# Key/value stage of a transformer block: the two LN1 norms and transposes of a tile pair placed behind products three and five of the value group instead of both behind product six

## The chip, the cores and the metric

The kernel runs on one core of one Trainium2 chip. The metric is device time in microseconds (us). The kernel before took 736.23 us (median of 3 runs, 735.11 to 737.95). The stage of interest is some 70 us long.

Engines are named as in the profile: PE (TensorE matmul), PEld (its weight load), DVE (VectorE), ACT (ScalarE), POOL (GpSimd), SP (the engine whose queue issues nearly all DMAs here).

## The reference

The block is a pre-norm linear attention followed by a pre-norm gated MLP, for 2048 tokens of width 1024, in bf16. Only the first lines matter here:

```
x = A_x                                    # [1, 2048, 1024]
h = x + A_ref(layernorm(x), wqkv, wo)      # linear attention, 32 heads
h2 = h + B_ref(layernorm(h), W_gate, W_up, W_down)

# in A_ref: q, k, v from layernorm(x) @ wqkv
pk = phi(k);  kv = sum over tokens of pk^T v;  z = sum of pk
```

## The kernel before

The tokens are 16 tiles of 128. The key/value stage works on pairs of tiles. For each pair it makes a product of the normalised tiles with the key weights and one with the value weights, each in seven half-size products (a Strassen-like scheme of sums and differences). The order of the seven in a group is P1, P7, P6, P2, P5, P4, P3; `hook(i)` stands behind the i-th product issued, so "behind product three" means hook 3.

```python
def sgroup(...):                       # one group; cuts marked ...
    prod(a, X(0, 0), W(0, 0), True, "P1");  ...;  hook(1)
    prod(f, SX(2), TW(2), True, "P7");      ...;  hook(2)
    prod(b, SX(1), TW(1), False, "P6");     ...;  hook(3)
    prod(a, X(1, 0), W(1, 0), False, "P2"); ...;  hook(4)
    prod(c, SX(0), TW(0), False, "P5")
    ident_act(sc, bank(c), ...)             # ACT copies a bank out
    s22 = e22(...);  s22[0]()               # value group: first value addition, DVE
    hook(5)
    prod(b, X(1, 1), TW(3), False, "P4")
    s21 = e21(...);  s21[0]()               # value group: second value addition, DVE
    hook(6)
    prod(c, SX(3), W(1, 1), False, "P3");   ...;  hook(7)
```

`SX` are sums and differences of the two transposed tiles of a pair, which DVE makes one pair ahead of its use:

```python
def x_sums(p, part=None):              # DVE, four operations of 128x512
    if part != 1: add(2, xb(0, 0), xb(0, 1), ALU.subtract, ...)  # reads both tiles of the pair
    ...
```

A tile is normalised by DVE into `xn`, transposed by a DMA into `xnT`, and its input slot is loaded again:

```python
def T1d(st):
    dma_t(sl_tx[k], xnT[:, :, st * P:(st + 1) * P], xn[:, k, :], ...)   # SP: DMA transpose
    if st + NX1 < NST:
        load_x1(st + NX1)                                               # SP: next x tile into the freed slot
def norm(st):
    if st < NST:
        ln1_norm(st)                   # DVE, 128x1024
        T1d(st)
def norms(p):
    norm(2 * p)
    norm(2 * p + 1)
```

The loop, with what stands in which hook:

```python
for p in range(NP_):
    # key group p: hook 1 ln1_stats(2p+6); hook 5 x_sums(p+2, 0) and ACT statistics; hook 6 x_sums(p+2, 1)
    k_group(p, hooks)
    if p + 2 < NP_:
        def v3(...):                   # behind product three of value group p+2
            ...
            if p == 0:
                x_sums(1)
                norm(6)
        def v5(p=p):                   # behind product five
            if p == 0:
                norm(7)
            ...                        # ACT statistics of tile 2p+9
        def v6(p=p, nq=nq):            # behind product six
            if p > 0:
                norms(p + 3)
            kvaccs(p)                  # 16 accumulating matmuls of 129 columns
            ...
        v_group(p + 2, {2: v2, 3: v3, 5: v5, 6: v6})
```

So the first pair (tiles 6 and 7) already had the new order. The pairs of p = 1 to 4 had both norms behind product six, and the next key group wants their transposed tiles behind its product five.

## Time and profile before

| what | before | view |
|---|---|---|
| span, granted clock | 734.9 us, 1.00 | the page |
| PE / DVE / ACT / POOL busy | 98 / 76 / 48 / 14% | the page |
| PE busy in the odd 14 us of the stage | 13.43 of 14.00 us | windows |
| a round on PE (accumulation to accumulation) | 13.16 to 13.21 us, but 13.61 in round 1 and 13.96 in round 3 | timeline |
| first transpose of the pair in that round | issued 64.07 us, landed after 3.1 us | timeline, DMA |
| second transpose | issued 65.97 us, landed after 4.8 us | timeline, DMA |

The sixteen narrow matmuls of an accumulation (128x129, from RE) are a good mark on PE's timeline. Successive starts of them give the rounds: 35.51, 49.12, 62.29, 76.25, 89.41 and 102.62 us, so rounds 1 to 5 take 13.61, 13.17, 13.96, 13.16 and 13.21 us.

PE's timeline of the kernel before (start, duration, engine, line, operation, tiles, count; in brackets the idle time before and who ended it):

```profile
62.29 1.10 PE L710 MATMUL ps<-RE 128*128 128x129 bf16 x16
63.44 0.81 PE L710 MATMUL ps<-RAB,RH 128*128 128x512 bf16 x3
64.09 1.03 PE L710 MATMUL ps<-RAB 128*128 128x512 bf16 x4
...
71.32 1.04 PE L710 MATMUL ps<-RW,RWG 128*128 128x512 f16 x4
72.81 1.02 PE L710 MATMUL ps<-RW,RWG 128*128 128x512 f16 x4 [0.45 <-DVE RWG L931]
...
76.25 1.10 PE L710 MATMUL ps<-RE 128*128 128x129 bf16 x16
```

The third line, at 64.09, is the first matmul of the next key group. The odd round is round 3 (62.29 to 76.25). In it PE stands idle for 0.45 us before a product that reads DVE's pair sum (L931), and the product before it started late as well.

The timeline of all engines of the kernel before, the lines of the two norms (L778, L838), the value additions (L1073), SP's issues (SPq) and the pair sum:

```profile
62.30 0.69 DVE L1073 TENSOR_TENSOR RE<-ps,RX 128x512 bf16<-128x512 f32 x1 [0.46 <-ACT RX L715]
62.91 0.68 DVE L1073 TENSOR_TENSOR RE<-ps,RXH 128x512 bf16<-128x512 f32 x1
63.51 0.54 DVE L778 TENSOR_SCALAR RXH<-RE,mv,rstd 128x1024 bf16<-128x1024 bf16 x1
63.96 0.54 DVE L838 TENSOR_SCALAR RXH<-RE,s 128x1024 bf16<-128x1024 bf16 x1
64.07 1.23 SPq L545 DMA_TRANSPOSE RAB<-RXH  x1
65.35 0.58 SPq L541 DMA_DIRECT2D RE<-in_A_x_dram  x1
65.97 1.23 SPq L545 DMA_TRANSPOSE RAB<-RXH  x1
...
70.84 0.42 DVE L931 TENSOR_TENSOR RWG<-RAB 128x512 f16<-128x512 bf16 x1 [0.81 <-DMA RAB<-RXH]
```

Two things are to be seen. The second norm is done at 64.50, but its transpose is issued only at 65.97, because SP first issues the other transpose and a load. And DVE stands 0.81 us at 70.84, released by the DMA of that transpose: it was ready at 70.03, which is +5.9 us on the round's clock. The chain of waits of the kernel before (start, duration, what) runs through just this:

```profile
65.97 4.84 DMA RAB<-RXH
70.82 0.02 issue
70.84 0.42 DVE RWG L931
```

### The profile page before, as it was taken

To read this page: it belongs to the slowest core of one execution; us is meant where nothing else is said; L and a number is where in the kernel's file an instruction comes from. 1 tells how busy PE (TensorE), PEld (TensorE's weight loads), DVE (VectorE), ACT (ScalarE), POOL (GpSimd) and SP (SyncE) were. 2 spreads that over 40 slices of the span, in tenths; PEclk is the share of its full clock that TensorE was granted. 3 is DMA by queue.
4 is the path that set the end of the run, shared out by engine and by line. 5 is a ranking of instruction groups with operands and counts; after the bars stand their busy time and mean duration, and the time that the engine had idled before them with its cause. 6 is when DMAs were issued, how large, how long until landed. Compare 5 with 4: busy or idle time off the path is not lost.

```text
span 734.9 us, 11505 instructions
## 1 busy us (share of the span) xinstructions
PE 720.8 (98%) x4253; PEld 363.2 (49%) x4311; DVE 561.6 (76%) x976; ACT 352.0 (48%) x614; POOL 103.7 (14%) x169
## 2 busy tenths in 40 slices
PE   8999999999999999999999999999999999999998
PEld 3444444344444444444444666754444444447766
DVE  7878877898775999898997769865757575667594
ACT  4877666764832456777754100135454544521000
POOL 1311100000450112132320003400000000000052
PEclk9999999999999999999999999999999999999999
DMA  9644154024999889888969999982323242327892
GB/s 313 202 91 83 29 142 157 3 30 75 214 228 260 234 258 272 241 243 256 300 198 305 318 247 336 311 263 79 101 71 109 63 116 58 100 92 245 246 314 87
DMA packets 191880, 133.93 MB, mean 182 GB/s; under 512 B 51664, under 2 KB 173776, under 8 KB 191824
## 3 DMA queue, kind: packets, MB, share of 16 engines
q1 hardware_dynamic: 191152, 132.54, 63.6%
q8 instruction: 34, 0.56, 0.3%
q10 hardware_dynamic: 672, 0.66, 0.3%
q14 instruction: 22, 0.18, 0.1%
HBM read 96.47 MB, written 25.17 MB: 166 GB/s over the span
## 4 chain that ended last, share of the span: by engine, by line
PE 82%; DVE 9%; DMA 3%; issue 2%; ACT 2%; SPq 1%; POOL 1%; POOLq 0%; DVEq 0%; ACTq 0%
PE ps L710 82%; DMA RW<-in_B_W_down_dram 1%; DVE RAB L796 1%; DVE RE L1171 1%; ACT RX L789 1%; DMA RX<-h_scr 1%; DVE st L724 1%; DMA RAB<-RXH 1%; DVE RX L793 1%; SPq L541 1%; DVE RX L1012 1%; DVE RO L1289 1%; POOL rstd L734 0%; DVE RW L906 0%; ACT ps L715 0%
## 5 line engine op out<-in xcount | busy, mean ns | idle before, releaser
L715 ACT ACTIVATE ps<-ps 128x512 f32<-128x512 f32 x172 | 100.1, 582 | 213.5 <-PE ps L710 162.0
L710 PE MATMUL ps<-RC,RO 128*128 128x512 f16 x672 | 154.3, 379 | 0.0
L710 PE MATMUL ps<-RH,RWG 128*128 128x512 bf16 x447 | 105.6, 379 | 0.1
L710 PEld LDWEIGHTS ps<-RC,RO 128*128 128x128 f16 x672 | 65.7, 98 | 79.5 <-ACT ps L715 0.5
L1345 DVE TENSOR_TENSOR RAB<-ps,RAB 128x512 bf16<-128x512 f32 x56 | 38.6, 689 | 71.9 <-PE ps L710 71.9
L710 PE MATMUL ps<-RC,RWG 128*128 128x512 f16 x320 | 76.8, 379 | 0.3 <-ACT ps L715 0.3
L1341 DVE TENSOR_TENSOR RE<-ps,RE 128x512 bf16<-128x512 f32 x112 | 74.2, 684 | 1.6 <-PE ps L710 0.7
L710 PEld LDWEIGHTS ps<-RH,RWG 128*128 128x128 bf16 x448 | 43.9, 98 | 52.6
L710 PE MATMUL ps<-RW,RAB 128*128 128x256 f16 (+3 forms) x412 | 66.8, 318 | 1.5 <-DVE RAB L1423 1.0
L1423 POOL TENSOR_TENSOR RE<-RE,RX 128x512 f32<-128x512 f32 x16 | 23.1, 1473 | 307.5 <-DMA RX<-h_scr 307.5
L715 ACT ACTIVATE RE<-RE 128x512 bf16<-128x512 bf16 x56 | 35.1, 627 | 65.0 <-DVE RE L1341 64.4
L710 PE MATMUL ps<-RH,RO 128*128 128x512 bf16 (+1 forms) x228 | 55.3, 379 | 3.0 <-DVE RE L1341 1.6
L710 PE MATMUL ps<-RW,RE 128*128 128x512 bf16 x243 | 56.6, 380 | 1.5 <-DVE RXH L1195 0.7
L710 PE MATMUL ps<-RAB 128*128 128x512 bf16 (+2 forms) x268 | 57.6, 351 | 0.4
L715 ACT ACTIVATE RE<-ps 128x512 f32<-128x512 f32 x64 | 37.6, 597 | 35.4 <-PE ps L710 35.0
L710 PEld LDWEIGHTS ps<-RW,RAB 128*128 128x128 bf16 (+1 forms) x414 | 40.4, 98 | 25.8 <-DVE RAB L1423 1.3
L710 PEld LDWEIGHTS ps<-RC,RWG 128*128 128x128 bf16 (+1 forms) x320 | 30.0, 98 | 40.2 <-ACT ps L715 6.2
L1289 DVE TENSOR_TENSOR RO<-RWG 128x1024 f16<-128x1024 bf16 x54 | 39.7, 736 | 4.7 <-DMA RWG<-in_B_W_up_dram 4.7
L1423 DVE TENSOR_TENSOR RE<-ps,RE 128x512 f32<-128x512 f32 x40 | 27.0, 687 | 18.9 <-PE ps L710 15.6
L715 ACT ACTIVATE RAB<-ps 128x512 bf16<-128x512 f32 x56 | 33.4, 596 | 14.7 <-PE ps L710 13.6
L710 PEld LDWEIGHTS ps<-RH,RO 128*128 128x128 f16 (+1 forms) x256 | 24.2, 98 | 31.8 <-DVE RE L1341 2.2
L710 PEld LDWEIGHTS ps<-RAB 128*128 128x128 bf16 (+1 forms) x274 | 26.3, 98 | 25.2 <-ACT RAB L856 1.1
(138 smaller groups left out, 994.0 us busy)
## 6 DMA issues: line engine op xcount, KB each, us to landing
RWG<-in_B_W_gate_dram SPq DMA_DIRECT2D x28, 512.0 KB, 5.0
RWG<-in_B_W_up_dram SPq DMA_DIRECT2D x28, 512.0 KB, 5.9
RW<-in_B_W_down_dram SPq DMA_DIRECT2D x14, 512.0 KB, 6.1
t_scr<-RW SPq DMA_DIRECT2D x14, 512.0 KB, 3.5
RE<-in_A_x_dram SPq DMA_DIRECT2D x23, 256.0 KB, 3.5
RW<-l_scr SPq DMA_DIRECT2D x13, 448.0 KB, 6.3
l_scr<-RX SPq DMA_DIRECT2D x7, 768.0 KB, 4.4
RW<-in_B_W_down_dram SPq DMA_DIRECT2D x12, 384.0 KB, 5.0
```

The source lines that it names most:

```text
L541: return PL.add(eng, lambda e: e.dma_start(dst_ap, src_ap), reads=reads, writes=writes, slot=slot, name=name)
L710: lambda e: e.matmul(out_ap, lhsT, rhs, start=start, stop=stop, skip_group_check=skip),
L715: PL.add("act", lambda e: e.activation(out=dst, in_=src, func=func), reads=reads, writes=writes, name=name)
L724: PL.add("dve", lambda e: e.bn_stats(out=st6[:, k, c * 6:(c + 1) * 6], in_=src_full[:, c * BCH:(c + 1) * BCH]), reads=[src_chunk_bufs[c]], ...
L789: PL.add("act", lambda e: e.activation(out=Et[:, k, :], in_=src, func=ACTF.Exp), reads=[src_buf], writes=[B_E[k]], name=name + "_exp")
L793: PL.add("dve", lambda e: e.tensor_scalar(out=Et[:, k, :], in0=Et[:, k, :], scalar1=1.0, scalar2=1e-6, op0=ALU.min, op1=ALU.add), reads=[] ...
L796: PL.add("dve", lambda e: e.scalar_tensor_tensor(out=dst_ap, in0=src, scalar=C1, in1=Et[:, k, :], op0=ALU.add, op1=ALU.max), reads=[src_bu ...
L1012: PL.add("dve", lambda e: e.tensor_tensor(out=s_, in0=p_, in1=s_, op=ALU.add), reads=[pb], writes=[sb_], name=name + "_add")
L1289: PL.add(eng, lambda e: e.tensor_tensor(out=tb(j, u), in0=f0(u), in1=f1(u), op=ALU.subtract), reads=[B_w[i + x] for x in r] + ([B_T[k + x] ...
L1341: PL.add("dve", lambda e: e.tensor_tensor(out=dst, in0=src, in1=ftmp[:, w, :], op=ALU.add), reads=[bsrc, B_s5[w]], writes=[bdst], name=name)
L1345: PL.add("dve", lambda e: e.tensor_tensor(out=dst, in0=a_, in1=b_, op=ALU.mult), reads=reads, writes=[wr], name=name)
L1423: PL.add(eng, lambda e: e.tensor_tensor(out=dst, in0=in0, in1=in1, op=op), reads=reads, writes=writes, name=name)
```

## The change

The intent: finish the norms earlier in the value group, so that the transposes start earlier, and fill DVE's wait for ACT ahead of the first value addition. No operation is added or removed.

```diff
                     if p == 0:
                         x_sums(1)
                         norm(6)
+                    else:
+                        norm(2 * p + 6)
 
                 def v5(p=p):
-                    if p == 0:
-                        norm(7)
+                    norm(2 * p + 7)
                     B = 2 * p + 9
 ...
                 def v6(p=p, nq=nq):
-                    if p > 0:
-                        norms(p + 3)
                     kvaccs(p)
```

## The prediction

> What bounds the kernel now. TensorE. The page gives PE 98% busy, DVE 76%, ACT 48%, POOL 14%. In the key/value stage (about 36 to 116 us of the 734.9 us span) the windows view shows PE busy 19.4 to 20.0 us of every 20 us and DVE 14.5 to 16.3. One round (key group, value group, accumulation) repeats on PE every 13.14 to 13.21 us (starts at 50.93, 64.09, 78.05, 91.21, 104.42), except one that takes 13.96 us. So there is little to gain but 0.8 us.
>
> The chain of waits and the timeline show the odd round. DVE makes two norms behind product six at 63.51 and 63.96 us (0.54 us each). SP issues the first transpose at 64.07 (1.23 us of issue), the load after it at 65.35 (0.58), the second transpose only at 65.97; it lands 4.84 us later, at 70.82 (minimum and median of these transposes 3.0 and 3.2 us). The pair sum of the next key group, ready to start at about 70.03, waits 0.81 us for it, and PE then stands at the product that reads the sum.
>
> What the change does. Nothing is added or removed: four pairs of norms with transposes and loads come earlier. The first pair has this order already. The first norm moves in front of the first value addition (L1073). There DVE now stands idle 0.36 to 0.48 us per round, waiting for ACT's copy, so the norm (0.45 us start to start) fills that hole. The second norm goes between the two value additions and delays the second by about 0.45 us. That addition releases a PSUM bank which the next key group needs only at its third product's copy, some 2 us later, and its value tile is read two pairs later; I count no PE time for it. The statistics are ready: POOL's last operation on them ends near 58.2 us, the norm would run at about 61.8.
>
> First norm 63.51 to about 61.9, issue 64.07 to about 62.4; second norm 63.96 to about 63.0, but SP is then busy until about 64.3, so the second issue moves from 65.97 to about 64.3, 1.6 us earlier. Even a landing of 4.84 us would end at about 69.2, before 70.03. The wait of 0.81 us should vanish, and with it 0.7 to 0.8 us of PE. The Trainium skill, "DMA: Bandwidth & Descriptors" (Anatomy of one DMA, there for GpSimd's path), puts a transfer's fixed part at about 2 us; this trace shows a floor too (3.0 us), so only an earlier issue helps.
>
> The other rounds show no such wait, so I expect 0 to 0.8 us in total, at most about 1.5 in executions with two late landings: about -0.6 us of 736.23; the three runs spread over 735.11 to 737.95.
>
> Predicted: 735.6 us, range 734.0 to 737.3. Chances: faster by over 2% 0.01, within 2% 0.98, slower by over 2% 0.01.
>
> What would show it: all rounds 13.1 to 13.2 us on PE; no DVE wait on the transposed tile; second transposes issued 1.6 us earlier; DVE's wait for ACT before the first value addition nearly gone; second value addition 0.5 us later with no new PE wait.
>
> What would make it wrong: the 4.84 us landing was chance and after has its own; the earlier loads slow the second transpose; the later second addition holds a bank and PE waits for ACT's copy, some 0.3 us per round, making it slower by about 1 us.

## The result, and the profile after

The changed kernel took 735.6 us (median of 6 runs, 734.91 to 737.83), the kernel before 736.35 us in its 6 runs (735.11 to 737.95). The ratio was 0.9994, with a 95% interval of 0.9976 to 1.0013. A ratio here is the mean time of one kernel's fast runs over that of the other's of the same rounds, so it is not quite the ratio of the medians. By time alone, no difference seen: the interval contains 1. A later set of runs (below) gave 0.9985, interval 0.9972 to 0.9998.

The profiled execution of the changed kernel happened to be the slowest of its six (737.83 us), and its span is 1.2 us longer than that of before. The stage must therefore be read by itself. PE's timeline of the changed kernel:

```profile
64.77 1.10 PE L710 MATMUL ps<-RE 128*128 128x129 bf16 x16
65.71 1.02 PE L710 MATMUL ps<-RAB,RH 128*128 128x512 bf16 x4
66.57 1.03 PE L710 MATMUL ps<-RAB 128*128 128x512 bf16 x4
...
73.56 1.94 PE L710 MATMUL ps<-RW,RWG 128*128 128x512 f16 x8
...
77.92 1.10 PE L710 MATMUL ps<-RE 128*128 128x129 bf16 x16
```

Round 3 now takes 13.15 us (64.77 to 77.92), and the two products that were torn apart in before run as one line of eight matmuls. All five rounds: 13.37, 13.17, 13.15, 13.16 and 13.21 us. The timeline of all engines, the lines that answer to those above:

```profile
64.24 0.54 DVE L778 TENSOR_SCALAR RXH<-RE,mv,rstd 128x1024 bf16<-128x1024 bf16 x1
64.78 0.69 DVE L1073 TENSOR_TENSOR RE<-ps,RX 128x512 bf16<-128x512 f32 x1
64.80 1.23 SPq L545 DMA_TRANSPOSE RAB<-RXH  x1
65.39 0.54 DVE L838 TENSOR_SCALAR RXH<-RE,s 128x1024 bf16<-128x1024 bf16 x1
65.84 0.68 DVE L1073 TENSOR_TENSOR RE<-ps,RXH 128x512 bf16<-128x512 f32 x1
66.08 0.58 SPq L541 DMA_DIRECT2D RE<-in_A_x_dram  x1
66.70 1.23 SPq L545 DMA_TRANSPOSE RAB<-RXH  x1
...
72.43 0.41 DVE L931 TENSOR_TENSOR RWG<-RAB 128x512 f16<-128x512 bf16 x1
```

The first norm fills the hole before the first value addition, which has no bracket any more. On the round's clock (zero at 66.57) the second transpose is issued at +0.13 us instead of +1.88. It lands at +3.7 us, over 2 us before it is wanted, and the pair sum waits for nothing. The windows view of 14 us around the round (length, then PE, PEld, DVE, ACT and POOL busy with counts, clock, DMA share, GB/s), first of before, then of after:

```profile
64.00:78.00 14.00, 13.43 (x73) 5.95 (x72) 10.87 (x25) 10.31 (x21) 1.78 (x5) 1.00 0.42 76
```

```profile
64.00:78.00 14.00, 14.00 (x79) 6.39 (x78) 11.57 (x26) 10.90 (x22) 1.96 (x5) 1.00 0.34 76
```

Where, then, did the 1.2 us of span come from? The first accumulation starts at 38.23 us in after and at 35.51 in before (+2.72). The five rounds take 66.06 us instead of 67.11 (-1.05: 0.81 in round 3 and 0.24 in round 1; the latter is scatter and not the change, since a repeat of the kernel before also had 13.36 us there). The rest of the program takes 631.8 us instead of 632.3 (-0.5). The start is the culprit, before any moved norm: in the changed kernel's profiled execution PE stood 1.90 us for the first norm (0.77 in before), and then ran with a lower granted clock. The windows from 8 to 18 us, before and then after:

```profile
8.00:18.00 10.00, 9.82 (x64) 4.93 (x64) 9.00 (x19) 5.65 (x12) 1.46 (x3) 1.00 1.09 355
```

```profile
8.00:18.00 10.00, 9.48 (x54) 4.82 (x55) 8.93 (x21) 4.73 (x9) 1.65 (x3) 0.83 1.09 357
```

A repeat of the changed kernel began its first accumulation at 35.90 us, so this late start is not a property of the change.

### The profile page after: what moved, and what is told of

Its sections match the earlier page's. It is cut to its first block, busy times and chain, and to the rows that moved or that the text cites. A ratio compares the mean times of both kernels' runs of the same rounds, so it can differ in the third digit from the quotient of the medians.

```text
span 736.1 us, 11563 instructions
## 1 busy us (share of the span) xinstructions
PE 725.6 (99%) x4311; PEld 364.0 (49%) x4311; DVE 561.1 (76%) x976; ACT 352.3 (48%) x614; POOL 105.5 (14%) x169
## 4 chain that ended last, share of the span: by engine, by line
PE 85%; DVE 8%; ACT 2%; DMA 2%; SPq 1%; issue 1%; POOL 0%; DVEq 0%; POOLq 0%; ACTq 0%
PE ps L710 84%; DVE RAB L1423 2%; DMA RW<-in_B_W_down_dram 1%; DVE RAB L796 1%; SPq L545 1%; ACT RX L789 1%; DVE RE L1171 1%; DMA RE<-in_A_x_dram 1%; DVE RX L793 1%; SPq L541 1%; DVE RO L1289 0%; ACT ps L715 0%; ACT RXH L748 0%; DVE RX L1012 0%; DVE RE L1423 0%
## 5 line engine op out<-in xcount | busy, mean ns | idle before, releaser
L710 PE MATMUL ps<-RW,RAB 128*128 128x256 f16 (+3 forms) x414 | 66.9, 318 | 1.3 <-DVE RAB L1423 0.8
L710 PE MATMUL ps<-RH,RO 128*128 128x512 bf16 (+1 forms) x256 | 61.3, 380 | 0.9 <-DVE RE L1341 0.9
L710 PE MATMUL ps<-RAB 128*128 128x512 bf16 (+2 forms) x274 | 59.3, 357 | 0.1
```

What stands on the lines that cost most here:

```text
L710: lambda e: e.matmul(out_ap, lhsT, rhs, start=start, stop=stop, skip_group_check=skip),
```

## The experiments

Theory: the second transpose lands at the edge of the moment when it is wanted, and PE pays for what is over. Rivals: the one late landing was chance and the change did nothing, or the gain has another source. A second question arose on the way: why is it always round 3? All profiled executions but that of late (a run described below) are collected in this table. Times marked + or - are us from the zero of round 3 (first matmul of the next key group); the sum wants both transposes at +5.9.

| kernel | second transpose issued | instruction fetch starts | second transpose landed | DVE wait | round 3 |
|---|---|---|---|---|---|
| before | +1.88 | +3.8 | +6.7 | 0.81 | 13.96 |
| before_again | +1.88 | +3.6 | +6.5 | 0.55 | 13.71 |
| second_only | +1.29 | +3.5 | +6.4 | 0.52 | 13.67 |
| loads_last | +1.27 | +3.4 | +5.9 | none | 13.15 |
| before_later | +1.88 | +4.4 | +7.3 | 1.34 | 14.50 |
| before_fetch | +1.88 | -1.3 | +5.4 | none | 13.16 |
| after | +0.13 | +3.8 | +3.7 | none | 13.15 |
| after_again | +0.14 | +3.9 | +3.7 | none | 13.15 |
| first_only | +0.14 | +2.9 | +3.7 | none | 13.16 |
| after_fetch | +0.80 | -0.5 | +4.2 | none | 13.16 |
| after_hit2 | +0.15 | +4.1 | +3.7 | none | 13.15 |
| after_hit4 | +0.14 | +0.3 | +4.3 | none | 13.15 |
| best | -0.48 | +4.0 | +2.7 | none | 13.16 |

The column of the fetch needs a word. The DMA view lists, beside the data queue, queues of kind "instruction"; that of the kernel before over the whole span (packets, MB, share of the 16 engines):

```profile
q8 instruction: 34, 0.56, 0.3%
q14 instruction: 22, 0.18, 0.1%
```

The Trainium skill, "Runtime: NRT & Kernel Launch" (Instruction fetch mechanics), says that an engine's instruction memory is refilled in blocks of 16 KiB, 256 instructions, through a DMA queue of its own. The numbers agree with q8 being PE's: the trace has 34 packets of 16 KB, and the page counts 4311 weight loads, each with a matmul, so 8622 instructions or 33.7 blocks. The table has q8's fetch. Its start was read by narrowing the window of the DMA view until the packet fell into 0.1 us. The other queue, q14, fetches 8 KB at a time, and did no such harm where it met a transpose: in best one of its fetches started 2.4 us after a transpose's issue (36.99 us), which landed after 3.65 us.

### before_again and after_again: is it chance?

The same two programs, profiled and timed once more, five rounds each.

> The kernel before, run and profiled again. Theory (the second transpose of a pair lands at the edge of its need; only a late landing costs PE time): some of the rounds that begin near 51, 64, 78 and 91 us may show a DVE wait of 0.1 to 1 us on the transposed tile, and a round of 13.15 us on PE is longer by just that wait; rounds without it take 13.14 to 13.21 us. Rival 1 (the 4.84 us landing was one accident): all landings near 3.2 us, no such wait. Rival 2 (systematic): the same round waits about 0.8 us again. Time against before: same, within 0.2%.

> The changed kernel again. Theory: no DVE wait on the transposed tile in any round, all PE rounds of the stage 13.14 to 13.21 us, second transpose issued about 0.13 us after the next key group's first matmul (1.88 us in before). Time 0.0 to 0.8 us under before (ratio 0.999 to 1.000), too little to be clear of the spread. Rival (the added wait of the second value addition costs PE time): rounds longer than 13.21 us.

Measured: before_again 736.54 us (6 runs; before 736.37, 11 runs), ratio 1.0005, interval 0.9992 to 1.0018. Round 3 again, and only round 3, had the wait: 13.71 us, with this line in the waits of DVE from 60 to 75 us:

```profile
DVE RWG L931 <- DMA RAB<-RXH: 0.5, 1, 0.5
```

after_again 735.38 us (5 runs), ratio 0.9985, interval 0.9972 to 0.9998; rounds 13.36, 13.15, 13.15, 13.16 and 13.20 us, no wait on the transposed tile. So the late landing is not an accident: two of two traces of before have it in the same round (rival 2 of before_again's text), and none of two of the changed kernel. The gain seen on PE is 0.55 to 0.8 us; the ratio's interval (0.15 to 2.1 us) holds that and is not finer.

### first_only: which half of the change does it?

```diff
                         norm(6)
+                    else:
+                        norm(2 * p + 6)
 ...                                     # v5 as before
                 def v6(p=p, nq=nq):
                     if p > 0:
-                        norms(p + 3)
+                        norm(2 * p + 7)
```

> Only the first norm of the pair moved (behind product three); the second stays behind six. Theory (the second transpose is held back by SP issuing the first transpose and the load, 1.23 + 0.67 us, not by its norm): second transpose issued at 0.1 to 0.2 us after the next key group's first matmul, as with both moved (before: 1.88), no wait on the transposed tile. Rival (its own norm holds it): issued near 1.3 to 1.9 us.

Measured (one look, 734.92 us): second transpose issued at +0.14 us, as with both moved; no wait; round 3 13.16 us. SP's timeline in it:

```profile
62.33 1.23 SPq L545 DMA_TRANSPOSE RAB<-RXH  x1
...
64.22 1.23 SPq L545 DMA_TRANSPOSE RAB<-RXH  x1
```

The second transpose was held back by SP's issue of the first one and of the load, not by its own norm. In this one trace, the half of the change that moves the second norm is worth nothing.

### second_only and loads_last: the same time from SP's side

second_only moves the second norm alone (behind product five); the first stays behind six, and the transposes change places. loads_last leaves the norms where before had them, and issues both loads behind both transposes.

```diff
 # second_only
-                    if p == 0:
-                        norm(7)
+                    norm(2 * p + 7)
 ...
                     if p > 0:
-                        norms(p + 3)
+                        norm(2 * p + 6)
```

```diff
 # loads_last
         def norms(p):
-            norm(2 * p)
-            norm(2 * p + 1)
+            for st in (2 * p, 2 * p + 1):
+                if st < NST:
+                    ln1_norm(st)
+                    T1d(st, False)            # transpose without the load
+            for st in (2 * p, 2 * p + 1):
+                if st + NX1 < NST:
+                    load_x1(st + NX1)
```

> Only the second norm moved (behind product five), the first stays behind six, so the two transposes change places. Theory (SP issues them one after the other with a load between, so the later of the two is issued 1.9 us after the first): first issue about 0.6 us before the next key group's first matmul, second about 1.2 to 1.3 us after it (before: 1.88), so at most a small wait in the third round (0 to 0.3 us), or none.

> Norms where before had them; the two loads of x are issued behind both transposes instead of one between them. Theory: second transpose issued about 1.3 us after the next key group's first matmul instead of 1.88 in the rounds that load; the wait in the third round shrinks from 0.5 to 0.8 us to 0 to 0.3 us. Rival (only the norms' place matters): wait as in before.

Measured (one look each, 737.12 and 737.55 us): the later transposes were issued at +1.29 and +1.27 us, as expected. The wait was 0.52 us in second_only, more than the 0 to 0.3 expected, since the landing stretched to 5.1 us; in loads_last there was none, the landing at +5.9 being just in time. So an earlier issue did not by itself bring an earlier landing: with issues at +1.88, +1.29 and +1.27 the landing came at +6.5 to +6.7, +6.4 and +5.9, always 2.5 to 2.9 us after the start of the fetch. The fetch is not the whole of it: second_only and loads_last had the same issue and fetches 0.1 us apart, yet landed 0.5 us apart. They differ in the place of the loads and in when the first transpose was issued (-0.61 and -0.01); which of these matters was not tested.

### late: what does a later transpose cost?

```diff
                 if p > 0 and A < NST:
                     ln1_stats(A)
+                if p > 1:
+                    norms(p + 2)          # in the next key group, behind its product one
 ...
                 def v6(p=p, nq=nq):
-                    if p > 0:
-                        norms(p + 3)
                     kvaccs(p)
```

> Both norms and transposes put later instead of earlier: behind the statistics in the next key group (after its product one), about 2.1 us later on DVE than in before where statistics stand there. Theory (landing has under 1 us to spare, and every us beyond goes to PE one to one): the sum waits about 2.3 us in each of the two rounds that also load x, 1.7 us in the next, under 0.5 us in the last, so 6 us slower in all (4 to 8), ratio about 1.008, with PE waiting for the sum. Rival (transposes are off the path, 0.8 us of the odd round had another cause): within 1 us of before, PE rounds unchanged.

Measured: 740.26 us (5 runs; before 736.37), ratio 1.0058, interval 1.0046 to 1.0070, so about 4.3 us slower, at the low end of the range. Rounds 2 to 5 took 14.53, 17.61, 13.90 and 13.20 us, where 13.15 to 13.2 is undisturbed: +1.4, +4.5, +0.7 and 0. The four rounds together are 5.7 and 6.0 us longer than those of the two traces of before, as expected; how that divides among them is not. In rounds 2 and 4 the sum waited 1.38 and 0.74 us, and PE lost just that. The traced run was the slowest of the five: it and one of 741.48 us had a mean granted clock of 0.998, while the other three, at 0.999 to 1.000, took 739.48 to 740.26 us. So a part of what the trace shows, most likely the loss of clock told next, is not in every run. The rival, within 1 us of before, is out. Round 3 is instructive. Its lines of DVE, PE and windows:

```profile
74.13 0.42 DVE L931 TENSOR_TENSOR RWG<-RAB 128x512 f16<-128x512 bf16 x1 [2.77 <-DMA RAB<-RXH]
```

```profile
71.55 1.03 PE L710 MATMUL ps<-RAB 128*128 128x512 bf16 x4
74.61 1.04 PE L710 MATMUL ps<-RW,RWG 128*128 128x512 f16 x4 [2.04 <-DVE RWG L931]
76.09 1.82 PE L710 MATMUL ps<-RW,RWG 128*128 128x512 f16 x4 [0.44 <-DVE RWG L931]
77.71 1.91 PE L710 MATMUL ps<-RAB 128*128 128x512 bf16 x4
```

```profile
74.00:82.00 8.00, 6.94 (x34) 3.07 (x35) 5.64 (x13) 3.68 (x6) 0.00 (x0) 0.79 0.02 8
```

The DVE wait of 2.77 us explains 2.8 of the 4.5 us. (About 1.1 us of this wait most likely goes back to a fetch again: it started 0.5 us after SP began to issue the first transpose, and that issue took 2.29 us instead of 1.23.) The rest is a second cost: after PE's pauses of 2.04 and 0.44 us the granted clock fell to 0.79 in this stretch, and groups of four matmuls that take 1.03 us took 1.82 and 1.91. In the packed trace the clock stands at one half for 3.41 us from 76.17 us on, which costs 1.7 us.

### before_fetch and before_later: why round 3?

A look at round 3 of before with the DMA view shows the one thing that only this round has: an instruction fetch of 16 KB, starting at 67.9 us, while the second transpose moves. (The fetches next to it start at 46.8 and 90.6 us; the pairs of transposes around them move from 37.0 to 42.5, from 50.9 to 56.6 and from 91.2 to 95.6 us.) The DMA view of before from 65.9 to 71.2 us (40 slices; busy tenths, then GB/s) and its line of the queue:

```profile
DMA  9999798002799999999900000000299998969400
GB/s 209 205 205 189 157 215 62 15 15 46 278 371 371 334 321 410 261 205 128 64 0 0 8 8 10 8 12 10 56 280 286 286 486 340 464 247 340 155 0 0
q8 instruction: 1, 0.02, 1.1%
```

From the 21st to the 28th slice (about 68.5 to 69.6 us) all 16 engines together moved 12 GB/s or less, and then the rest of the transpose went through. The fetch's own packet is 1.1% of 16 engines' 5.3 us, so 0.9 us on one engine; how it can quiet all sixteen, for longer than it lasts itself, no run shows. To move the fetch without moving a norm, the number of matmuls at the program's start was changed, which shifts the block boundaries:

```diff
 # before_fetch: 22 matmuls more
-        pe_dummies(12, P1_POOL)
+        pe_dummies(9, P1_POOL)
+        for i in range(25):
+            b = P1_POOL[i % 5]
+            mm(bank(b, 8), zeros_t[:, 0:P], zeros_t[:, 0:8], True, True, ...)
 # before_later: 4 matmuls fewer
-        pe_dummies(12, P1_POOL)
+        pe_dummies(8, P1_POOL)
```

> The kernel before, norms where they were; only 22 more matmuls stand at the start (9 dummies of 512 columns and 25 of 8 instead of 12 of 512), so that PE's fetch of 16 KB of instructions, which in both runs of before starts about 1.9 us after the second transpose of the third round is issued (67.9 and 67.4 us), comes about 4 us earlier in that round. Theory (the late landing of 4.6 to 4.8 us is this transpose held up by the fetch): second transpose of that round lands in 3.5 to 3.8 us, no DVE wait on the transposed tile, PE round 13.15 to 13.2 us instead of 13.71 to 13.96; time like that of the change, 0.5 to 1 us under before. Rival (the landing is late for something else at that place, the load or the address): 4.6 to 4.8 us and a wait again.

> The kernel before with 4 dummy matmuls fewer at the start, so that PE's fetch of the third round comes about 0.9 us later against that round (times from the next key group's first matmul: fetch at about +4.5 instead of +3.6 to +3.8; second transpose issued at +1.88, landing undisturbed at about +5.4, wanted at about +5.9). Theory (a fetch that starts while the transpose moves puts its landing at the fetch's start + 2.6 to 2.9 us, as in before, its repeat, second_only and loads_last): landing at about +7.3, DVE wait about 1.4 us, PE round about 14.5 us. Rival (the late landing has a fixed size): landing +6.5 to +6.7, round 13.7 to 14.0.

Measured in before_fetch: fetch at -1.3 us; the same transpose, issued at the same +1.88, landed after 3.5 us, at 70.15; no wait; round 3 13.16 us. Its issue and the pair sum, which has no bracket:

```profile
66.61 1.23 SPq L545 DMA_TRANSPOSE RAB<-RXH  x1
...
70.58 0.42 DVE L931 TENSOR_TENSOR RWG<-RAB 128x512 f16<-128x512 bf16 x1
```

Measured in before_later (one look): fetch at +4.4, landing after 5.4 us at +7.3, and these lines, the pair sum on DVE and the DMA view from 66.9 to 72.4 us:

```profile
72.30 0.42 DVE L931 TENSOR_TENSOR RWG<-RAB 128x512 f16<-128x512 bf16 x1 [1.34 <-DMA RAB<-RXH]
```

```profile
GB/s 214 212 188 194 179 194 104 45 15 119 223 387 365 278 296 268 244 141 142 0 0 0 0 0 4 7 9 9 9 9 11 236 296 290 394 417 477 238 343 135
```

Wait and round (1.34 and 14.50 us) are what was written down, 1.4 and 14.5 (the 2.6 us of that text, which was loads_last, is 2.5 when read again); the lull in the traffic moved along with the fetch and grew to 12 slices, 1.65 us. With the norms in place, moving only PE's instruction count took the wait away in one direction and nearly doubled it in the other, so the fetch is shown, by one trace each way, to be the cause of the late landing. Not borne out was the time: before_fetch took 736.17 us (6 runs; before 736.41, 11 runs), ratio 1.0003, interval 0.9988 to 1.0018, though 0.5 to 1 us less was expected (the interval does not exclude that). In its trace the first accumulation starts at 36.40 us, against 35.51 and 35.49 in the two traces of before, which would eat the gain. PE ran at a lower clock for longer there: the packed trace has full clock only from 9.99 us on, the other thirteen from 4.34 to 7.35 us, and three matmuls of 512 columns at 7.73 us took 1.49 us, against 0.81 in before. Whether the added matmuls do that or the scatter of the start (35.49 to 38.23 us over all traces) is open.

### after_fetch, after_hit2 and after_hit4: is the change only lucky?

In the two traces of the changed kernel the fetch starts 0.1 to 0.25 us after the second transpose has landed. Is the change worth something only because it slips past the fetch? These move the fetch in the changed kernel in the same way (11 wide and 11 tiny dummies; 12 wide and 2 tiny; 12 wide and 4 tiny).

> The changed kernel with 10 more matmuls at the start, so that PE's fetch in the third round, which there starts 3.6 to 3.8 us after the second transpose's issue (just past its landing), comes about 1.8 us earlier, into the transpose. Theory: that transpose lands in 4.4 to 4.9 us instead of 3.5, but with no DVE wait and no longer round on PE, since it is issued 1.75 us earlier than in before: round 13.15 to 13.2 us. Rival (the gain of the change is only that it moved out of the fetch's way): a DVE wait of some tenths of a us on the tile and a round over 13.5 us.

> The changed kernel with 2 tiny matmuls more at the start, so that the fetch, which in its two traces starts at +3.82 and +3.89 us, 0.1 to 0.25 us after the second transpose has landed, comes about 0.4 us earlier, at +3.4 or so. Theory (start + 2.6 to 2.9 us if it catches the transpose): landing at about +6.0 to +6.3, a wait of 0.1 to 0.4 us and a round up to 13.5 us; the change is then worth less, but still more than nothing. Rival (moved early, the transpose is past the part that a fetch can hold up, as the fetch at +2.88 in first_only was): landing under +4, no wait, round 13.15 us.

> The changed kernel with 4 tiny matmuls more at the start: fetch at about +3.0 us, in the middle of the second transpose. Theory: landing at most at about +5.9 us, just in time, no wait, round 13.15 us. Rival (the change only dodges the fetch): wait and round as in before, 13.7 to 14.0 us.

Measured (one look each, 737.07, 735.93 and 735.08 us): none has a wait, and all three rounds are 13.15 to 13.16 us. But the fetch did not go where it was aimed: to -0.5, +4.1 and +0.3 us instead of about +2, +3.4 and +3.0. It shifts in jumps that the count of matmuls alone does not tell. So these runs do not test the worst case, a fetch into the last part of the transpose. In after_fetch and after_hit4 it caught the first transpose (landing after 4.1 and 4.5 us), and the second was still 1.6 us early or more.

What is left is an estimate from the table. In the five traces with the late landing the fetch started 1.7 to 2.5 us after the second transpose's issue, and the landing followed 2.5 to 2.9 us after the fetch. A fetch 2.75 us after the issue (first_only) held up nothing, and one 0.2 us after it (after_hit4) let it land after 4.2 us. In the changed kernel the latest harmful fetch would thus start at about 0.14 + 2.75 = +2.9 us and the landing would follow at about +5.8, 0.1 us before it is wanted. In before the same sum gives 1.88 + 2.75 + 2.9 = +7.5, that is 1.6 us of wait. By this estimate the earlier issue just protects the round wherever the fetch falls; no run shows that last step.

### best: what the experiments point to

The changed kernel, with both loads of a pair behind the second transpose, and three slots instead of two for the statistics that ACT makes. In round 1 ACT's statistics of tile 9 have to wait until norm 6 has read the slot that they overwrite (1.3 to 1.6 us of ACT), and PE then waits for a copy by ACT.

```diff
-        s1 = sb("s1", [P, 2, 4], f32)
+        s1 = sb("s1", [P, 3, 4], f32)
 ...
-            k = len(ln1_a) % 2
+            k = len(ln1_a) % 3
 ...
         def norm(st):
             if st < NST:
                 ln1_norm(st)
-                T1d(st)
+                T1d(st, False)
 ...
                     norm(2 * p + 7)
+                    for st in (2 * p + 6, 2 * p + 7):
+                        if st + NX1 < NST:
+                            load_x1(st + NX1)
```

> The changed kernel with both loads of x behind the second transpose, and three slots instead of two for ACT's statistics, so that the statistics of tile 9 need not wait until norm 6 has read its slot. Expected: second transpose issued about 0.5 us before the next key group's first matmul (changed kernel: 0.13 after), landing well before the fetch at +3.8; ACT's wait for the norm in the round before (1.3 to 1.6 us) gone and with it the 0.2 to 0.4 us that PE waits for ACT in the second round, whose PE time becomes 13.15 to 13.2 us instead of 13.36 to 13.65. Time 0.2 to 0.4 us under the changed kernel, 1.0 to 1.5 under before (ratio about 0.9983), at the edge of what five rounds show.

(The "second round" of that text is round 1 of the count used here.) Measured: 735.14 us (6 runs; before 735.95, 11 runs), ratio 0.9986, interval 0.9972 to 1.0000. Its traced rounds are 13.16, 13.15, 13.16, 13.16 and 13.21 us: round 1, 13.36 to 13.65 in every other trace, is now as short as the rest, and the second transpose is issued at -0.48 us. About 0.3 us of this was lost again in the trace after the fifth round (14.40 us to the next accumulation, 14.11 to 14.12 in before and after), for a reason not looked into. By time it is ahead of before at the edge of what can be seen, and it is not to be told from the changed kernel.

## Why the prediction was right

It gave 735.6 us and a range of 734.0 to 737.3; measured were 735.6 and, in the second set, 735.38. That the number fits to 0.1 us is luck: the medians of before alone run from 735.95 to 736.41 over the sets of 11 runs, and a kernel without any gain would have fallen into the range as well. What bears the prediction out is its mechanism, as the traces show it.

- **Bound and place of the loss.** Right. In the traces of before, of the changed kernel and of their repeats, rounds 2, 4 and 5 take 13.15 to 13.21 us, and the change could only take the 0.5 to 0.8 us of round 3. Round 1, at 13.36 to 13.61 us, had a loss of its own that the prediction missed (best points to ACT's statistics); the change does not touch that loss.
- **The first norm fills DVE's hole.** Right. The hole of 0.46 us before the first value addition is gone, and the second addition starts 0.45 us later on the round's clock (63.48 - 64.21 = -0.73 in after_again, 62.91 - 64.09 = -1.18 in before). No PE wait came of it.
- **SP's issue decides the second transpose.** Right, and sharper than predicted: +0.13 us where the prediction's 64.3 means about +0.2; first_only shows that the second norm's move adds nothing.
- **The size.** The wait of 0.81 us was taken from one trace; the repeat had 0.55, so the worth on PE is 0.55 to 0.8 us. The 0.6 us of the prediction lies in it. The times alone give -0.06% and -0.15%, each with an interval of about 0.13 to 0.19% to either side.
- **One step had the wrong form.** The prediction took 4.84 us as a duration that could recur wherever the transpose is issued ("Even a landing of 4.84 us would end at about 69.2"), and left open whether it was chance. It is neither. The landing follows the start of an instruction fetch by 2.5 to 2.9 us, if the fetch comes in the right part of the transpose (1.7 to 2.5 us after its issue). In second_only an issue 0.6 us earlier brought a landing only 0.1 to 0.4 us earlier. The conclusion held since the changed kernel's transpose has landed before the fetch starts.
- **The skill's floor.** The prediction cites "DMA: Bandwidth & Descriptors" (Anatomy of one DMA) for a fixed part of about 2 us and drew from it that only an earlier issue helps. The traces agree that there is a floor (3.0 us in every kernel), but before_fetch shows a second remedy: keep the other traffic away.

## What to carry to other kernels

When a DMA that is issued well ahead lands late in one place and on time in four like places, look for what else uses the DMA engines at that moment, and count the instruction fetches in; their place depends on the program's instruction count, so an unrelated edit can move such a wait. An earlier issue is a remedy that depends less on where the fetch falls, and where several DMAs go through one issuing queue, the order and cost of the issues (here 1.9 us for a transpose and a load) can matter more than when their data are ready. With effects under 0.2% of the time, compare the rounds of a stage in the trace: the scatter of the start alone (35.5 to 38.2 us) was several times the gain.

## What the Trainium skill lacked or had wrong

- "Runtime: NRT & Kernel Launch" (Instruction fetch mechanics) calls the cost of crossing a 16 KiB boundary "mostly hidden". For PE's own stream no run contradicts that, but the fetch is not free for the other DMAs: a transpose under way landed after 4.6 to 5.4 us instead of 3.5, with 1.06 us (before) and 1.65 us (before_later) in which all the DMA engines together moved 12 GB/s or less, and PE lost 0.5 to 1.3 us through it.
- No page gives what a fetch does to a DMA's issue. SP took 2.29 us instead of 1.23 for one transpose around a fetch (late), and 1.23 instead of 0.58 us for a load (after_fetch). The changed kernel had it too: in round 5 of both its traces a fetch started 0.5 to 0.6 us after SP began the pair's first transpose, whose issue took 1.90 and 2.06 us.
- "DMA: Bandwidth & Descriptors" (Issuing engines are not separate DMA queues) says that the time to start a DMA is usually small beside the DMA itself. Here a transpose of a 128x1024 bf16 tile occupied SP for 1.23 us against 3.0 to 3.8 us from issue to landing where no fetch met it, and a pair's second transpose was issued 1.9 us after the first because of it and of a load.
- "TensorE: Matmul & The Clock Gate" (Part 1) lets the clock fall after about 3.4 us of idleness. In late the granted clock fell to 0.79 after a pause of 2.04 us and one of 0.44, and at the start of the changed kernel's profiled run to 0.83 after one of 1.90 us. The measurements decide: shorter pauses than that cost clock. In the packed traces the clock stands at one half for 3.41 us in all four mid-run cases, after 3.41 us in which PE had stood for 1.90 (after), 2.11 (before_later), 2.25 (loads_last) and 2.30 us (late) in all; 1.68 us (start of after_fetch) and 1.99 us (end of late) were not followed by a fall, so these traces give no sharp limit.
